# Sliding-window attention and a SiLU MLP on one core: transposes as 32x32 blocks on VectorE, matmuls in four small tiles

## The chip, the core and the metric

The kernel runs on one core of one Trainium2 chip. A core has TensorE (PE: matmuls, and its weight loads, PEld), VectorE (DVE), ScalarE (ACT), GpSimd (POOL) and SyncE (SP); POOL and SP issue DMAs to and from the chip's memory, POOL those that also cast float32 to bfloat16. Matmul results go to PSUM, here eight banks of 512 float32 for each of 128 partitions; everything else lies in SBUF. The metric is the device time of one execution in microseconds (us), as the median of several runs.

## The reference

Eight batches of eight heads, 576 positions, head size 64; a position attends to itself and the 63 before it. The result, all heads side by side, is the input of an MLP of 512, 2048 and 512 features.

```python
scores = scale * np.matmul(q, k.transpose(0, 1, 3, 2))          # scale = 1/8
mask = (rel >= 0) & (rel < window)                              # window = 64
scores = np.where(mask, scores, -1000000000.0)
attn = np.exp(scores - np.max(scores, axis=-1, keepdims=True))
attn = attn / (np.sum(attn, axis=-1, keepdims=True) + 1e-09)
x = np.matmul(attn, v).transpose(0, 2, 1, 3).reshape(B * S, H * D)   # 4608 x 512
h = x @ w_in
out = (h * (1.0 / (1.0 + np.exp(-h)))) @ w_out
```

## The kernel before

**Layout.** TensorE contracts over partitions, so q and k are needed with the head's 64 features on partitions (`qt`, `kt`), and the attention result O, which comes out with positions on partitions, must be turned again for the first MLP layer (`bridge`: features on partitions, 72 blocks of 64 positions). The kernel therefore transposes q, k and O, in three ways:

- Batch 0: `turn_first` (L294) transposes q and k on TensorE, `lift` copies them out of PSUM.
- Batch 1: `load_cast` loads a pair of heads (147 KB as bfloat16), `turn_twos` (L306, matmuls at L310) transposes on TensorE, `lift_twos` (L319) copies out in four quarters, on ACT or DVE.
- Batches 2 to 7 (`NX = 2`): `load_raw` loads pairs into `nat` (L259), `turn_raw` (L261) has SP issue a DMA that transposes two pairs into `tt`, and `spread` (L265) copies each quarter on DVE to its place, 32 copies per batch.
- O: `normal` (L385) divides by the row sums. Up to batch 2's second group, and in one group of batch 3, `back` (L388, matmuls at L390) transposes on TensorE and `to_bridge` (L399, L401) copies out; all other groups use `turn_o` (L393), a transposing DMA from SP.

**Attention.** A unit is one batch, three blocks of 64 queries (`g`, 0 to 2), and four heads (`a`, 0 or 1; "half") or all eight ("whole", batches 2 to 7). `scores` (L344, matmuls L350) multiplies 128 keys by 64 queries over 64 features; the two heads of a pair lie on partitions 0 to 63 and 64 to 127, so the array is used as two tiles of 64 rows. `expo` (L364) takes exp on ACT, `masking` (L367) multiplies by the window on DVE (in batch 0 a bias is added on TensorE instead, L358). `values` (L369, matmuls L373) has the 64 queries of two heads in two tiles of 64 columns, with a column of ones in `vv` for the row sum; `inverse` (L379) takes its reciprocal. `shift_v` (L333, L335) copies v so that each window of 128 keys has its own place.

**MLP.** Nine tiles of 512 positions. `first_layer` (L406): 16 groups of 128 features by 4 contractions; `silu` (L412) on ACT; `second_layer` (L415): 4 blocks of 128 positions by 16 contractions; `copy_out` (L421) and `store`. In tile 0 the first `FIRST = 6` groups are cut into 192 and 320 positions, since the first 192 are ready first, and the second layer takes the contractions in the outer loop, as w_out arrives.

**Order.** No order is written by hand: `Plan` (L12) is a planner that runs before the program is emitted. Each operation has a class with a rank, the engines that may take it with their estimated times, what it depends on, and the PSUM banks that it needs (`at` for scores, `pv` for values, `mp` for the MLP). The planner plays the program through with these times and emits each engine's operations in the order found; on the chip an engine executes its own in that order and waits where something is late. Scores are admitted by `scores_may_run` (L436): a whole unit only in a second layer with more than 14 of its 64 matmuls left. The DMA operations' times (`dma=`) are estimates of the same kind. `warm` (L668) keeps TensorE busy until the first batch's exps.

Of the kernel before, what the change touches and what calls it, by code (L numbers as in the profile page):

```python
# [14 lines left out]
class Plan:  # L15
# [12 lines left out]
    def add(self, cls, us, fn, deps=(), lat=0.08, gate=None, dma=None, pool=None, table=None, b=0, nb=1):  # L28
        if b > 1 and cls in ("cast", "lift", "spread", "mask", "norm"):
            lat = 0.2  # L30
        op = dict(us=us, first=self.rank[cls] + b if b or cls not in self.rank0 else self.rank0[cls], fn=fn, deps=[d for d in deps if d is not None], lat=lat, gate=gate, dma=dma,
                  pool=pool, table=table, seen=None, n=self.count, untils=[[] for _ in range(nb)], bank=[])
        self.count += 1
        self.queues.setdefault(cls, []).append(op)
        return op
# [87 lines left out]
def kernel(ctx, tc, q, k, v, w_in, w_out, out):  # L123
# [6 lines left out]
    NM = 6  # L130
    NR = S // NM
# [7 lines left out]
    NN, NNB, NTS, NE, NOT, NGT = 5, 8, 4, 12, 4, NFT + 3  # L139
    FIRST, EARLY_OUT = 6, 1  # L140
    FIRST_LOADS = [(x[0], int(x[1])) for x in "q0 k0 q1 k1 q2 q3 k2 k3 v0 v1 v2 v3".split()]
    NX, NXO = 2, 3
    NOX, NRC, NV = 4, 6, 3
# [18 lines left out]
    nats = [keep.tile([128, 2 * NM * 128], BF16, name=f"nat{i}") for i in range(NN)]  # L162
    tts = [keep.tile([128, 2 * S], BF16, name=f"tt{i}") for i in range(NTS)]
    natbs = [keep.tile([128, 2 * NM * D], BF16, name=f"natb{i}") for i in range(NNB)]
# [4 lines left out]
    rcs = [keep.tile([128, 2, 3], FP32, name=f"rc{i}") for i in range(NRC)]  # L169
    oxs = [keep.tile([128, 3, 2, 128], BF16, name=f"ox{i}") for i in range(NOX)]  # L170
# [10 lines left out]
        rank=dict(prime=-8, early=-10, one=-9, first=-9, dma=-1, ld0=-1, ld1=-1, st=-2, xo=-1.5, xk=-1.4, silu=-3, out=-2, pv=0, ot=0, s=1, moe=99, warm=200, turn=2,  # L181
                  norm=0, inverse=0, bridge=0, exp=1, mask=1, lift=2, spread=2, shift=2, cast=4, late=5, clear=9),
        rank0=dict(turn=-6, cast=-6, lift=-5, shift=-4.5, exp=-4, mask=-4, inverse=-3.5, norm=-3, bridge=-3.2),
        ahead=dict(s=-5.5, exp=-4.6, pv=-5.5, inverse=-4.3, norm=-4.2, ot=-5.5, bridge=-4.25),
# [44 lines left out]
    def head(pj, hh):  # L229
        return 4 * (pj // 2) + 2 * hh + pj % 2  # L230

    def pair(b, pj, kk):
        return (q, k)[kk][b, head(pj, 0):head(pj, 1) + 1:2]

    def two(u, kk):
        return (q, k)[kk][0, 2 * u:2 * u + 2].rearrange("h s d -> (h s) d").rearrange("(p m) d -> p (m d)", m=NM0)

    def load_cast(w, b, pj, kk):

        nc.gpsimd.dma_start(  # L240
            out=natbs[w][0:NR].rearrange("p (h y) -> p h y", h=2),
            in_=pair(b, pj, kk).rearrange("h (p m) d -> p h (m d)", m=NM),
        )
# [11 lines left out]
    def raw(i):  # L255
        return nats[i][0:NR].rearrange("p (j h y) -> p j h y", j=2, h=2)

    def load_raw(i, b, pj, kk):
        nc.gpsimd.dma_start(out=raw(i)[:, pj % 2], in_=pair(b, pj, kk).rearrange("h (p m) d -> p h (m d)", m=NM))  # L259

    def turn_raw(i, t):  # L261
        nc.sync.dma_start_transpose(  # L262
            out=tts[t].rearrange("x (m p) -> x m p", m=2 * NM), in_=nats[i][0:NR])

    def spread(e, t, b, pj, kk, hh, r):  # L265
        copies[e](  # L266
            out=place_one(b, pj, kk)[64 * hh:64 * hh + 64].rearrange("x (p m) -> x p m", m=NM)[:, :, r::2],
            in_=tts[t][64 * r:64 * r + 64].rearrange("x (j h m p) -> x j h p m", j=2, h=2, m=NM // 2)[:, pj % 2, hh],
        )
# [8 lines left out]
    def load_w_in(f):  # L278
        nc.gpsimd.dma_start(
            out=w_in_sb[:, :, f * 256:(f + 1) * 256],  # L280
            in_=w_in[:, f * 256:(f + 1) * 256].rearrange("(c p) f -> p c f", p=128),
        )
# [23 lines left out]
    def turn_twos(op, w):  # L306

        pst = at_bf16(op).rearrange("x (m p) -> x m p", m=NM)
        for m in range(NM):
            nc.tensor.matmul(  # L310
                pst[:, m], lhsT=natbs[w][0:NR, 128 * m:128 * m + 128], rhs=ident[0:NR, 0:NR],
                is_transpose=True, start=(m == 0), stop=(m == NM - 1),
            )

    def place_one(b, pj, kk):
        return kt[b % NK][:, 64 + pj * S:64 + (pj + 1) * S] if kk else qt[b % NK][:, pj * S:(pj + 1) * S]

    def lift_twos(e, op, b, pj, kk, hh, r):
        copies[e](  # L319
            out=place_one(b, pj, kk)[64 * hh:64 * hh + 64].rearrange("x (p m) -> x p m", m=NM)[:, :, r::2],  # L320
            in_=at_bf16(op)[64 * r:64 * r + 64].rearrange("x (h m p) -> x h p m", h=2, m=NM // 2)[:, hh],
        )
# [18 lines left out]
    def at_pv(bank):  # L341
        return banks[bank][:, 0:6 * (D + 1)].rearrange("k (j x y) -> k j x y", j=2, x=3)

    def scores(op, b, a, g, of):  # L344
        for j in range(2):
            for x in range(3):
                at = (2 * a + j) * S + (3 * g + x) * 64
                for hh in range(2):
                    r = slice(64 * hh, 64 * hh + 64)
                    nc.tensor.matmul(  # L350
                        at_six(of[hh])[:, j, x], lhsT=kt[b % NK][r, at:at + 128], rhs=qt[b % NK][r, at:at + 64],
                        start=(b > 0 and j == x == 0), stop=(j == 1 and x == 2),
                    )

    def scores_idle(op, b, a, g, of):

        for hh in range(2):
            nc.tensor.matmul(  # L358
                banks[of[hh]][:, 0:384], lhsT=ident,
                rhs=(bias0 if g == 0 else bias).rearrange("k x h i -> k (x h i)"), start=True, stop=False)  # L360
        scores(op, b, a, g, of)
# [6 lines left out]

    def values(bank, b, a, g, n):  # L369
        for j in range(2):  # L370
            for x in range(3):
                for hh in range(2):
                    nc.tensor.matmul(  # L373
                        at_pv(bank)[64 * hh:64 * hh + 64, j, x], lhsT=es[(2 * n + hh) % NE][:, j, x],
                        rhs=vv[b % NV][:, head(2 * a + j, hh) * NB + 3 * g + x, 0:D + 1],
                        start=(j == x == 0), stop=(j == 1 and x == 2),
# [5 lines left out]
    def ox(n):  # L382
        return oxs[n // 2 % NOX][:, :, n % 2].rearrange("k x (j d) -> k j x d", j=2)

    def normal(e, bank, n):  # L385
        nc.vector.tensor_mul(ox(n), at_pv(bank)[:, :, :, 0:D], rcs[n % NRC].unsqueeze(3).to_broadcast([128, 2, 3, D]))  # L386

    def back(bank, n):  # L388
        for x in range(3):
            nc.tensor.matmul(banks[bank][:, 128 * x:128 * x + 128], lhsT=oxs[n // 2 % NOX][:, x, n % 2], rhs=ident,  # L390
                             start=(x == 0), stop=(x == 2))

    def turn_o(n, b, g):  # L393
        n0 = b * NB + 3 * g
        nc.sync.dma_start_transpose(
            out=bridge[:, n0:n0 + 3].rearrange("x t (a h) i -> x (t a) (h i)", a=2),
            in_=oxs[n // 2 % NOX].rearrange("i t a x -> i (t a x)"))

    def to_bridge(e, bank, b, a, g):  # L399
        n0 = b * NB + 3 * g  # L400
        copies[e](out=bridge[:, n0:n0 + 3, 2 * a:2 * a + 2].rearrange("x t h i -> x t (h i)"),  # L401
                  in_=banks[bank][:, 0:384].rearrange("x (t y) -> x t y", t=3))
# [28 lines left out]
    nat_free, natb_free, tt_free, n_tt = {}, {}, {}, [0]  # L431
    g_pv, g_norm, g_back, g_mask, o_done = [], [], [], [], {}
# [15 lines left out]
    def add_first_batch():  # L448
        got = {}
        for what, u in FIRST_LOADS:  # L450
# [6 lines left out]
            if u == 0:  # L457
# [4 lines left out]
                nat_free[i] = ca  # L462
# [9 lines left out]
            for i in range(2):  # L472
# [3 lines left out]
                kq_done[(0, x)] = kq_done.get((0, x), []) + tu["untils"][i]  # L476
            for w in ws:
                natb_free[w] = tu
# [4 lines left out]
    def add_batch_qk(b):  # L483
        pool = "at"
        slot, parts = {}, {0: [], 1: []}
        for pj in range(NP):
            kq_done[(b, pj)] = []
        for pj in range(NP):
            busy = s_last.get((b - NK, pj), []) + ([c_k[b % NK]] if b < NK else [])
            for kk in range(2):  # L490
                if b >= NX:
                    if pj % 2 == 0:
                        slot[kk] = n_nat[0] % NN
                        n_nat[0] += 1
                    i = slot[kk]
                    parts[kk] += [p.add("dma", {"POOL": 0.66}, lambda _, i=i, pj=pj, kk=kk: load_raw(i, b, pj, kk),
                                        [nat_free.get(i)], dma=0.65, lat=MARGIN)]
                    if pj % 2 == 0:
                        continue
                    t = n_tt[0] % NTS  # L500
                    n_tt[0] += 1
                    x = p.add("xk", {"SP": 1.4}, lambda _, i=i, t=t: turn_raw(i, t), parts[kk] + tt_free.get(t, []), dma=2.2)
                    nat_free[i] = x
                    parts[kk], tt_free[t] = [], []
                    for y in (pj - 1, pj):
                        for hh, r in [(0, 0), (0, 1), (1, 0), (1, 1)]:
                            kq_done[(b, y)].append(p.add(
# [216 lines left out]
```

## Time and profile before

| | |
|---|---|
| median of 3 runs | 319.32 us (318.86 to 319.51) |
| the profiled execution, its own time | 313.79 us |
| its span, first to last instruction | 312.0 us |
| mean granted TensorE clock | 0.995 |
| busy: PE, DVE, ACT, POOL | 294.3, 156.0, 179.6, 85.1 us |
| moved by DMA | 38.53 MB |

The profile is of one execution. Its page gives each engine's busy time; the span in 40 slices of 7.8 us, each digit a share in tenths; groups of instructions by source line as "line engine operation, written<-read, shapes, count | busy us, mean ns of one | idle us before them and what ended it". The timeline gives start, duration and count of merged instructions, with the idle time before them in brackets. "PEclk" is the share of its full clock that TensorE was granted. The chain of waits is followed back from the last instruction.

### The profile page before, as it was taken

The page shows a single profiled execution, that of the slowest core. Times are in us where ns is not written, and L with a number is a line of the kernel's source. Part 1 is how long each engine was busy: PE and PEld are TensorE (multiplying, and loading weights), DVE is VectorE, ACT ScalarE, POOL GpSimd, SP SyncE. Part 2 cuts the span into 40 slices and gives each one's busy share as a digit, 9 for nine tenths or more (in the row PEclk, how much of TensorE's full clock was granted, in tenths as well). Part 3 has the DMA queues.
Part 4 walks back from the last instruction along what each step waited for, and adds up shares of the span by engine and source line. Part 5 has one row for each costly group of instructions (what it writes and reads, how often), then busy time and mean ns, then how long its engine had stood idle before and what let it go on. Part 6 is the DMA issues. An engine that isn't in the chain of part 4 may idle for free.

```text
span 312.0 us, 6619 instructions
## 1 busy us (share of the span) xinstructions
PE 294.3 (94%) x2603; PEld 145.9 (47%) x2633; DVE 156.0 (50%) x443; ACT 179.6 (58%) x330; POOL 85.1 (27%) x119
## 2 busy tenths in 40 slices
PE   4999989999979999999959999999999999999996
PEld 2566445444534454445424455445544444444444
DVE  2481776696599888986995188716500000000000
ACT  4788976666528753776346745775375146316611
POOL 8947846283260832095500000000000000000000
PEclk9999999999999999999979999999999999999999
DMA  8999999999999999999999033103320110010011
GB/s 165 167 197 182 165 203 161 160 276 156 156 235 171 157 185 177 174 223 148 191 200 196 3 109 99 33 0 97 84 59 2 67 67 3 34 67 34 2 65 69
DMA packets 102494, 38.53 MB, mean 123 GB/s; under 512 B 79680, under 2 KB 97728, under 8 KB 102464
## 3 DMA queue, kind: packets, MB, share of 16 engines
q0 software_dynamic: 56288, 18.06, 56.3%
q1 hardware_dynamic: 46176, 20.06, 32.9%
q8 instruction: 20, 0.33, 0.4%
q14 instruction: 10, 0.08, 0.1%
HBM read 36.70 MB, written 9.44 MB: 148 GB/s over the span
## 4 chain that ended last, share of the span: by engine, by line
PE 66%; DMA 24%; issue 3%; DVE 2%; POOL 2%; SPq 1%; ACT 0%; POOLq 0%; DVEq 0%; ACTq 0%
PE mp L406 32%; PE mp L415 27%; DMA vv<-in_v_dram 8%; DMA bridge<-ox 7%; DMA tt<-nat 3%; DMA nat<-in_q_dram 3%; DMA w_out_sb<-in_moe_w_out_dram 2%; PE mp L373 2%; PE at L350 2%; DMA natb<-in_q_dram 1%; POOL vv L273 1%; SPq L262 1%; PE at L300 1%; DVE ox L386 1%; PE mp L358 1%
## 5 line engine op out<-in xcount | busy, mean ns | idle before, releaser
L406 PE MATMUL mp<-bridge,w_in_sb 128*128 128x512 bf16 (+2 forms) x600 | 130.6, 372 | 3.7 <-DMA bridge<-ox 3.3
L415 PE MATMUL mp<-w_out_sb,g 128*128 128x512 bf16 (+2 forms) x578 | 128.9, 368 | 3.0 <-issue 2.2
L412 ACT ACTIVATE g<-mp 128x512 bf16<-128x512 f32 (+2 forms) x150 | 85.4, 580 | 36.3 <-PE mp L406 35.1
L406 PEld LDWEIGHTS <-w_in_sb 128*128 128x128 bf16 x600 | 57.6, 98 | 71.8 <-issue 8.3
L415 PEld LDWEIGHTS <-g 128*128 128x128 bf16 x608 | 55.5, 98 | 58.4 <-issue 0.5
L421 ACT COPY ot<-mp 128x512 f32<-128x512 f32 (+2 forms) x33 | 18.4, 560 | 62.7 <-PE mp L415 37.2
L364 ACT ACTIVATE e<-at 128x384 bf16<-128x384 f32 x88 | 36.8, 495 | 16.0 <-PE at L350 14.9
L367 DVE TENSOR_TENSOR e<-e,mask 128x384 bf16<-128x384 bf16 x84 | 26.9, 352 | 19.8 <-ACT e L364 19.3
L273 POOL DMA_DIRECT2D vv<-in_v_dram x32 | 32.6, 1026 | 8.8 <-DVE rc L380 4.7
L266 DVE COPY qt<-tt 64x288 bf16<-64x288 bf16 x96 | 33.6, 350 | 2.3 <-DMA tt<-nat 0.9
L266 DVE COPY kt<-tt 64x288 bf16<-64x288 bf16 x96 | 33.6, 350 | 1.8
L259 POOL DMA_DIRECT2D nat<-in_k_dram x24 | 15.6, 652 | 45.0 <-DMA tt<-nat 39.9
L386 DVE TENSOR_TENSOR ox<-mp,rc 128x384 bf16<-128x384 f32 x37 | 18.6, 542 | 0.2
L259 POOL DMA_DIRECT2D nat<-in_q_dram x24 | 15.8, 660 | 9.2 <-DMA tt<-nat 5.8
L373 PEld LDWEIGHTS <-e 128*64 128x64 bf16 x576 | 11.4, 110 | 10.5 <-issue 6.6
L350 PEld LDWEIGHTS <-kt 64*128 64x128 bf16 x576 | 10.2, 95 | 6.8 <-issue 4.7
L350 PE MATMUL at<-qt,kt 64*128 64x64 bf16 x528 | 13.0, 191 | 0.1
L380 DVE RECIPROCAL rc<-mp 128x6 f32<-128x6 f32 x37 | 6.8, 192 | 12.0 <-PE mp L373 11.9
L335 DVE COPY vv<-vv 64x576 bf16<-64x576 bf16 (+1 forms) x14 | 7.7, 549 | 6.6 <-DMA vv<-in_v_dram 6.1
L373 PE MATMUL mp<-vv,e 128*64 128x65 bf16 x444 | 10.7, 196 | 0.0
L412 ACT ACT_TABLE_LOAD x6 | 7.7, 1283 | 0.4 <-PE mp L406 0.3
L364 ACT ACT_TABLE_LOAD x6 | 7.7, 1283 | 0.1
(61 smaller groups left out, 123.1 us busy)
## 6 DMA issues: line engine op xcount, KB each, us to landing
out_dram<-ot SPq DMA_DIRECT2D x35, 256.0 KB, 2.2
vv<-in_v_dram POOLq DMA_DIRECT2D x32, 144.0 KB, 8.2
nat<-in_q_dram POOLq DMA_DIRECT2D x24, 144.0 KB, 8.6
nat<-in_k_dram POOLq DMA_DIRECT2D x24, 144.0 KB, 7.9
w_in_sb<-in_moe_w_in_dram POOLq DMA_DIRECT2D x8, 256.0 KB, 9.4
w_out_sb<-in_moe_w_out_dram POOLq DMA_DIRECT2D x8, 256.0 KB, 7.3
natb<-in_q_dram POOLq DMA_DIRECT2D x7, 144.0 KB, 6.2
natb<-in_k_dram POOLq DMA_DIRECT2D x7, 144.0 KB, 6.1
```

Of the source, the lines that this page charges most:

```text
L259: nc.gpsimd.dma_start(out=raw(i)[:, pj % 2], in_=pair(b, pj, kk).rearrange("h (p m) d -> p h (m d)", m=NM))
L266: copies[e](out=place_one(b, pj, kk)[64 * hh:64 * hh + 64].rearrange("x (p m) -> x p m", m=NM)[:, :, r::2], in_=tts[t][64 * r:64 * r + 64] ...
L273: queue[e].dma_start(out=vv[b % NV][:, 2 * g0 + 1:2 * g1 + 1:2, 0:D], in_=v[b].rearrange("h s d -> (h s) d").rearrange("(g p) d -> p g d", ...
L350: nc.tensor.matmul(at_six(of[hh])[:, j, x], lhsT=kt[b % NK][r, at:at + 128], rhs=qt[b % NK][r, at:at + 64], start=(b > 0 and j == x == 0), ...
L364: nc.scalar.activation(out=es[n % NE], in_=at_six(bank), func=ACTF.Exp, scale=scale)
L367: nc.vector.tensor_mul(es[n % NE], es[n % NE], mask0 if g == 0 else mask)
L373: nc.tensor.matmul(at_pv(bank)[64 * hh:64 * hh + 64, j, x], lhsT=es[(2 * n + hh) % NE][:, j, x], rhs=vv[b % NV][:, head(2 * a + j, hh) * N ...
L386: nc.vector.tensor_mul(ox(n), at_pv(bank)[:, :, :, 0:D], rcs[n % NRC].unsqueeze(3).to_broadcast([128, 2, 3, D]))
L406: nc.tensor.matmul(banks[bank["bank"][0]][:, lo:hi], lhsT=w_in_sb[:, c, ft * 128:(ft + 1) * 128], rhs=bridge[:, (j * TT + lo) // 64:(j * T ...
L412: nc.scalar.activation(out=gts[gt][:, lo:hi], in_=banks[bank["bank"][0]][:, lo:hi], func=ACTF.Silu)
L415: nc.tensor.matmul(banks[bank["bank"][0]][:, 0:hi - lo], lhsT=gts[gt][:, m * 128:(m + 1) * 128], rhs=w_out_sb[:, f, lo:hi], start=(f == 0) ...
L421: copies[e](out=ots[ot][:, lo:hi], in_=banks[bank["bank"][0]][:, 0:hi - lo])
```

## The change

- q and k of batches 1 to 7 are loaded by `load_four`: four heads at once, 128 partitions with 1152 consecutive elements (18 positions of 64 features) each, so that a head lies on a quarter of 32 partitions. `turn_blocks` turns 32x32 blocks on VectorE, half a load (576 elements) in each of two instructions per load. Then a head has 32 of its features (s = 0, 1) on its 32 partitions at a time.
- `scores` contracts 32 features twice, in four tiles of 32 rows, a head and a PSUM bank each: 48 matmuls per whole unit instead of 24.
- `values` takes 32 queries at a time in four tiles of 32 columns, a head each: also 48. O then has a head on 32 partitions, and `to_bridge` turns 32x32 blocks of it on VectorE, 384 elements, into `bridge`. This holds for batch 0 too.
- Gone: `load_cast`, `turn_twos`, `lift_twos`, `load_raw`, `turn_raw`, `spread`, `back`, `turn_o`, and with them all transposing DMAs and the batches' special ways.
- In `bridge` a partition now has features 2p and 2p + 1 of a half in the two places of that half, so w_in is loaded in the same order, in ten loads instead of eight.
- Batch 1 has whole units. FIRST is 8. The loads of batch 1's v and of w_out are issued in the order of `SECOND_LOADS`. Buffers: 8 `nat` of half the size, 6 `ox`.

The diff, cut to its core:

```diff
-    NN, NNB, NTS, NE, NOT, NGT = 5, 8, 4, 12, 4, NFT + 3
-    FIRST, EARLY_OUT = 6, 1
+    NN, NNB, NE, NOT, NGT = 8, 8, 12, 4, NFT + 3
+    FIRST, SECOND_LOADS = 8, "wvvwvv"
-    NX, NXO = 2, 3
-    NOX, NRC, NV = 4, 6, 3
+    NOX, NRC, NV = 6, 6, 3
...
+    def load_four(i, b, a, kk):
+        nc.gpsimd.dma_start(
+            out=nats[i], in_=(q, k)[kk][b, 4 * a:4 * a + 4].rearrange("h s d -> (h s d)").rearrange("(p x) -> p x", p=128))
+
+    def turn_blocks(i, b, a, kk, part):
+        n = NR // 2
+        to = kt[b % NK][:, 64:] if kk else qt[b % NK]
+        nc.vector.transpose(
+            out=to[:, 2 * a * S:2 * a * S + 2 * S].rearrange("x (s t r) -> x r s t", s=2, r=NR)[:, n * part:n * part + n],
+            in_=nats[i].rearrange("p (r s d) -> p r s d", r=NR, s=2)[:, n * part:n * part + n],
         )
...
-    def load_w_in(f):
+    def load_w_in(a, lo, hi):
         nc.gpsimd.dma_start(
-            out=w_in_sb[:, :, f * 256:(f + 1) * 256],
-            in_=w_in[:, f * 256:(f + 1) * 256].rearrange("(c p) f -> p c f", p=128),
+            out=w_in_sb[:, 2 * a:2 * a + 2, lo:hi],
+            in_=w_in[256 * a:256 * a + 256, lo:hi].rearrange("(p s) f -> p s f", s=2),
         )
...
+    def scores(op, b, g):
+        for s in range(2):
+            for a in range(2):
+                for x in range(3):
+                    at = (2 * a + s) * S + (3 * g + x) * 64
+                    for h in range(4):
+                        r = slice(32 * h, 32 * h + 32)
+                        nc.tensor.matmul(
+                            at_six(op["bank"][h])[:, a, x], lhsT=kt[b % NK][r, at:at + 128], rhs=qt[b % NK][r, at:at + 64],
+                            start=(s == a == x == 0), stop=(s == a == 1 and x == 2),
+                        )
...
     def values(bank, b, a, g, n):
-        for j in range(2):
-            for x in range(3):
-                for hh in range(2):
+        for x in range(3):
+            for t in range(2):
+                for h in range(4):
                     nc.tensor.matmul(
-                        at_pv(bank)[64 * hh:64 * hh + 64, j, x], lhsT=es[(2 * n + hh) % NE][:, j, x],
-                        rhs=vv[b % NV][:, head(2 * a + j, hh) * NB + 3 * g + x, 0:D + 1],
-                        start=(j == x == 0), stop=(j == 1 and x == 2),
+                        at_pv(bank)[32 * h:32 * h + 32, x, t], lhsT=e_of(b, a, n, h)[:, x, 32 * t:32 * t + 32],
+                        rhs=vv[b % NV][:, (4 * a + h) * NB + 3 * g + x, 0:D + 1],
+                        start=(x == t == 0), stop=(x == 2 and t == 1),
                     )
...
+    def to_bridge(n, b, a, g):
         n0 = b * NB + 3 * g
+        nc.vector.transpose(
+            out=bridge[:, n0:n0 + 3, 2 * a:2 * a + 2].rearrange("x t s (u i) -> x t s u i", u=2),
+            in_=oxs[n % NOX].rearrange("p t u (d s) -> p t s u d", s=2))
...
+                ld = p.add("dma", {"POOL": 0.66}, lambda _, i=i, a=a, kk=kk: load_four(i, b, a, kk), nat_free.get(i, []),
+                           dma=1.7, lat=MARGIN)
+                nat_free[i] = [p.add("block", {"DVE": 0.7}, lambda _, i=i, a=a, kk=kk, part=part: turn_blocks(i, b, a, kk, part),
+                                     [ld] + busy, b=b) for part in range(2)]
+                kq_done[(b, a)] += nat_free[i]
...
-        whole = b > 1
+        whole = b > 0
...
+            br = p.add("bridge" + first, {"DVE": 0.5}, lambda _, n=n, a=a: to_bridge(n, b, a, g), [no], b=b)
```

## The prediction

> **What bounds the kernel now.** I read the page first, busy shares and the slices of the span.
>
> ```profile
> PE 294.3 (94%) x2603; PEld 145.9 (47%) x2633; DVE 156.0 (50%) x443; ACT 179.6 (58%) x330; POOL 85.1 (27%) x119
> ...
> PE   4999989999979999999959999999999999999996
> ...
> DVE  2481776696599888986995188716500000000000
> ...
> DMA  8999999999999999999999033103320110010011
> ```
>
> TensorE is the bound: its row is full from the third slice on, with a dip in slice 12 (about 86 us) and in slice 21 (about 156 us). VectorE is at eight and nine tenths only up to slice 21, and the DMA engines are full exactly as long. So what counts is what TensorE executes, and its waits. The useful work is the two MLP layers:
>
> ```profile
> L406 PE MATMUL mp<-bridge,w_in_sb 128*128 128x512 bf16 (+2 forms) x600 | 130.6, 372 | 3.7 <-DMA bridge<-ox 3.3
> L415 PE MATMUL mp<-w_out_sb,g 128*128 128x512 bf16 (+2 forms) x578 | 128.9, 368 | 3.0 <-issue 2.2
> ```
>
> The 372 ns is the latency of one; in the chain of waits 64 of L406 take 13.99 us, 0.219 us each. The nine tiles need 1152 of these (some are cut in parts): 252 us. The first begins at 20.5, and 3 us follow the last. The other 36 us of the span are attention on TensorE, transposes on TensorE, and waits. The timeline of TensorE gives the waits:
>
> ```profile
> 40.97 0.41 PE L310 MATMUL at<-ident,natb 96*128 96x96 bf16 x6 [0.85 <-DVE kt L319]
> ...
> 88.01 0.34 PE L390 MATMUL mp<-ident,ox 128*128 128x128 bf16 x3 [1.88 <-DVE ox L386]
> ...
> 159.27 1.03 PE L406 MATMUL mp<-bridge,w_in_sb 128*128 128x512 bf16 x2 [3.29 <-DMA bridge<-ox]
> ```
>
> All three stand at things that the change replaces. The second is VectorE behind a late load of v (the chain has 16.8 us for that v load, from 68.78 on). The last also lowers the clock: windows, with the columns PE, PEld, DVE, ACT and POOL busy, clock, DMA share, GB/s:
>
> ```profile
> 155.00:170.00 15.00, 11.71 (x70) 5.20 (x70) 12.11 (x36) 7.73 (x12) 0.73 (x1) 0.89 1.52 196
> 170.00:185.00 15.00, 14.63 (x175) 7.34 (x176) 6.45 (x21) 9.92 (x20) 0.00 (x0) 1.00 0.24 56
> ```
>
> The list of waits tells why loads run to 170 us: buffers that wait for a transpose by DMA.
>
> ```profile
> POOL nat L259 <- DMA tt<-nat: 45.6, 10, 10.2
> ```
>
> [...] with transposes in flight, a load of v took 16.8 us where the median is 8.2. [...] The trace shows two abreast: in a prologue unit the two halves start at 15.00 and 15.00, 15.04 and 15.04, 15.06 and 15.07. Four abreast no run here shows. [...]
>
> **The change part by part.** The sum is made on the profiled execution, 313.79 us (span 312.0 and 1.8 around it). The median of the runs is 319.32, 5.5 above; I carry that offset unchanged.
>
> *TensorE work removed.* Turns of batch 1 (L310): 8 bursts, each 0.25 from its start to the next matmul: 2.0, and the 0.85 wait before the last. Turns of O (L390): 14 of the 18 groups lie after the first L406, each 0.17: 2.4. The 4 earlier ones and their copies lie in the prologue, replaced by VectorE below. Batch 1 has six half units now (scores 1.6, values 1.9 us in the burst starts) and then three whole ones. A whole unit costs 1.04: the tile from 192.74 to 224.90 has 32.16, less 128 x 0.219 = 28.0, over 4 units. 3.5 - 3.1 = 0.4.
>
> *Waits removed.* 1.88 and 3.29. And the clock: the 64 of L406 after the long wait take 15.45, where 14.0 is usual: 1.4. What is late next? A tile waits for the norm and one VectorE transpose in place of a DMA of 4.2 median and 12.5 at most, and in steady state units run ahead: when the fifth tile starts at 159.27, ten units of batches 2 to 4 have been scored and eight are needed. I expect nothing in that place.
>
> *VectorE.* Out: 192 copies L266 of 0.35 (67.2), its share of L319 (8.2) and L401 (3.4). In: 56 block turns of 576 elements and 48 bridge turns of 384. Price: [...] the estimates are 0.65 and 0.45 us. Sum 36.4 + 21.6 = 58, so VectorE falls from 156 to about 135. Bounds: [...] twice as slow if the writes 36 bytes apart halve it. Per later batch then: 8 x 0.65 turns, masks 12 x 0.35, inverses 6 x 0.19, norms 6 x 0.54, bridge turns 6 x 0.45, shifts 1.5: 18 us in 31 of TensorE, and 25 at the upper bound. So on the mean nothing, because 28 us of MLP per tile hide it; without that cover it would be 58 us. Queued behind a block turn that waits for its load are masks, and the values wait for those; a turn of 0.65 delays a mask by that much at most, against 3 to 4 us between score bursts.
>
> *Four tiles.* Scores and values are 48 matmuls each per unit instead of 24. Now 24 of L350 take 0.35 in 12 rounds of 29 ns, 24 of L373 in 12 rounds of 31. Four abreast is again 12 rounds: lower bound 0. Two abreast is 24 rounds: 12 x (29 + 31) ns x 21 units = 15.3 us. One at a time 46. I take four abreast with rounds some 2 ns longer: 1.0.
>
> *DMA.* The 24 + 15 transposes and their 10.0 MB of the 38.5 go, from SP, which then has only stores. q and k come in 4 loads per batch of twice the size, freed by VectorE instead of by a DMA; the 45.6 us of POOL's wait go. Before 48 us no transpose runs and DMA moves 165 to 200 GB/s, so the beginning gets no faster: the bytes up to batch 1 and w_out are the same. w_in in 10 loads instead of 8 costs POOL 2 x 0.75, behind which batch 1's loads stand; [...] From both: 0.4.
>
> *Prologue and first tile.* The last norm before the first L406 ends at 19.88; then come 0.35 on TensorE and a copy of 0.56. A transpose of 0.45 replaces both, but VectorE also takes the other half's copy, which ScalarE made: zero. FIRST = 8 cuts 8 matmuls more in two (101 + 136 instead of 219 ns): 0.15; it covers 3.2 us in which VectorE has four more norms and turns. Then the hand-over: first layer 20.5 + 14.6 + 0.3 = 35.4, second 14.0 + 3.1, so tile 1 could start at 52.5 (now 58.08). Batch 1's data are there at about 39 as now, units follow each other by 4.2 (179.82, 184.12, 188.21), so the third is scored at 47.4, and 5.8 later (exps and masks 2.5, values 0.5, inverses, norms, two turns 2.4, and waits) its last turn ends: 53.2. I take 1.0 as a new wait, from 0 to 3.5.
>
> Sum: 2.0 + 0.85 + 2.4 + 0.4 + 1.88 + 3.29 + 1.4 = 12.2 saved; 1.0 + 0.4 + 0.15 + 1.0 = 2.55 paid; 9.65 less. Profiled 304.1, median 309.7.
>
> **Rivals.** (1) The gain goes into new waits: TensorE's order is fixed by the planner, and where a VectorE turn comes later than planned, TensorE stands as it did at 88.01. For it: all three waits above are of this kind, and batch 1 as whole units leaves no slack in tile 0. Against: after tile 1 VectorE is lighter and units run ahead. With the hand-over at 3.5 and some 0.25 at each of 21 units: 8 given back, 317.5.
> (2) The small tiles do not run four abreast; this ends slower. Its place is the 42 bursts of scores and values. It decides when a round exceeds 29 to 31 by 10.65 us / (21 x 24 rounds) = 21 ns, at some 51 ns. Two abreast: 309.7 - 1.0 + 15.3 = 324.0. For it: column tiles of 32 and row tiles of 32 appear nowhere in this trace, and 8 instructions must issue in a round. Against: the pair's instructions start 1.5 to 4 ns apart in a 29 ns round, so eight fit.
> (3) The transposes on DMA were hidden and only the TensorE work counts: 2.0 + 0.85 + 2.4 + 0.4 - 2.55 = 3.1, 316.2. Against: the wait of 3.29 names one.
>
> **How the numbers follow.** Forecast 0.66 (303.5 to 314), rivals (1) and (3) together 0.17 (314 to 320), rival (2) 0.14 (over 320), more gain than I see 0.03. The range 303.5 to 319.0 leaves out some 0.18. The three runs differ by 0.2%, which is about what can be told from no change. Faster: 0.66 + 0.03 + 0.11 = 0.80; same 0.04; slower, rival (2) and the rest of (1), 0.16.
>
> **What would show it.** 48 of the scores' matmuls in 0.35 to 0.5 us, and the same for values; if 0.7 or more, rival (2). No wait of TensorE over 1 us after 60 us, clock 1.00 in every window from there; otherwise (1). VectorE's turns near 0.65 and 0.45, its total near 135. DMA idle from some 130 us or earlier, no POOL waits of 10 us. First L406 at 20 to 21, tile 1's first at 52.5 to 56. A much longer start of batch 1 (its scores after 42) would prove the DMA term wrong.

## The result, and the profile after

The changed kernel takes 354.45 us in the median of four runs (350.66 to 354.69); the kernel before took 319.41 beside it (318.86 to 320.95). The ratio is 1.106 (1.098 to 1.114): slower by a tenth, where 309.7 was forecast. An execution more than 1.5% above the fastest of the same kernel counts as slow, and the ratios leave such executions out, so they are not always the ratio of the medians. The profiled execution took 354.69 us, with a span of 352.9.

The page of the changed kernel, with the busy shares, the slices of the span, and the chain of waits by engine:

```profile
PE 305.3 (87%) x3619; PEld 147.8 (42%) x3619; DVE 233.8 (66%) x328; ACT 172.4 (49%) x311; POOL 65.1 (18%) x93
...
PE   5959456989406999699989998999999999999996
...
DVE  2648985999999699959998999699760262000000
...
PEclk9969969899855999789999998999999999999999
DMA  8999999363933192509451900100020011011002
...
PE 46%; DVE 28%; issue 11%; DMA 7%; POOL 6%; ACT 1%; POOLq 0%; DVEq 0%; ACTq 0%
```

VectorE was to fall from 156 to about 135 us; it rose to 233.8. It is mostly full from the eighth slice (62 us) to the 27th, and TensorE has a hole in slices 11 and 12 (88 to 106 us) and shallower ones before and after it. The DMA engines are full only in the first seven slices (to 62 us, where it was 171 before) and move 28.62 MB instead of 38.53, as the change says, and no wait of TensorE in this profile ends with a transfer. The groups of that page, with idle time and its releasers at the end of each row, tell what fills VectorE:

```profile
L371 PE MATMUL mp<-bridge,w_in_sb 128*128 128x512 bf16 (+2 forms) x608 | 130.5, 372 | 2.4 <-DVE ot L386 1.2
...
L247 DVE STREAM_TRANSPOSE qt<-nat 128x576 bf16<-128x576 bf16 x28 | 72.9, 2780 | 2.1 <-DMA nat<-in_q_dram 2.1
L247 DVE STREAM_TRANSPOSE kt<-nat 128x576 bf16<-128x576 bf16 x28 | 73.2, 2777 | 0.0
...
L351 PE MATMUL mp<-vv,e 128*32 128x65 bf16 x888 | 13.8, 200 | 22.4 <-DVE e L342 21.8
...
L365 DVE STREAM_TRANSPOSE bridge<-ox 128x384 bf16<-128x384 bf16 x48 | 24.8, 553 | 0.1
...
L333 PE MATMUL at<-qt,kt 32*128 32x64 bf16 x1008 | 13.0, 196 | 9.0 <-DVE kt L247 8.6
```

The bridge turns have nearly the forecast size: their median distance is 0.49 us from start to start, where 0.45 was forecast. A block turn has 2.78 us as its own latency and 2.47 from one start to the next, not 0.65; the 56 of them take 138 us, not 36. The MLP's matmuls are unchanged at 372 ns. The timeline of the changed kernel around the largest hole (start, duration, engine, instruction, count; in brackets the idle time before it and what ended it) shows how VectorE's time becomes TensorE's:

```profile
87.13 0.55 PE L333 MATMUL at<-qt,kt 32*128 32x64 bf16 x48
...
88.72 5.11 DVE L247 STREAM_TRANSPOSE qt<-nat 128x576 bf16<-128x576 bf16 x2
89.20 1.64 ACT L339 ACTIVATE e<-at 128x384 bf16<-128x384 f32 x4
93.48 5.27 DVE L247 STREAM_TRANSPOSE kt<-nat 128x576 bf16<-128x576 bf16 x2
...
98.40 5.27 DVE L247 STREAM_TRANSPOSE qt<-nat 128x576 bf16<-128x576 bf16 x2
...
103.32 5.27 DVE L247 STREAM_TRANSPOSE kt<-nat 128x576 bf16<-128x576 bf16 x2
...
108.24 1.33 DVE L342 TENSOR_TENSOR e<-e,mask 128x384 bf16<-128x384 bf16 x4
...
108.83 1.63 PE L351 MATMUL mp<-vv,e 128*32 128x65 bf16 x48 [16.73 <-DVE e L342]
```

The exps of a unit of batch 2 are done at 90.8. Its masks are emitted behind eight block turns of batch 3, which last 19.5 us; the planner counted 0.7 us for each, 5.6. TensorE stands 16.73 us before the values can start. The windows of the changed kernel, with busy PE, PEld, DVE, ACT, POOL, clock, DMA share and GB/s, give the price in clock as well:

```profile
90.00:110.00 20.00, 3.18 (x42) 1.46 (x43) 19.57 (x12) 1.43 (x4) 4.45 (x7) 0.63 0.83 92
110.00:125.00 15.00, 15.00 (x272) 7.29 (x261) 11.99 (x24) 4.72 (x11) 1.41 (x2) 0.81 0.23 58
```

TensorE is busy throughout the second window, at 0.81 of its clock. Over the whole span its stops of more than 0.1 us between matmuls sum to 39.9 us (9.6 before), and it is busy for 11 us more (305.3 against 294.3) although its transposes are gone; in run 2 below, with the same matmuls and a mean clock of 0.989 instead of 0.932, it is busy for 292.1. To within 0.4 us the longer stops (30.3) and the 11 us make the 40.9 by which the span grew. The list of waits of the changed kernel (waiter, what it waited for, total, count, longest) has them by cause:

```profile
POOL nat L240 <- DVE kt L247: 38.1, 8, 7.0
...
PE mp L351 <- DVE e L342: 21.8, 4, 16.7
...
PE at L333 <- DVE kt L247: 8.6, 1, 8.6
...
PE at L351 <- issue: 6.8, 2, 4.3
```

Three of these are VectorE's turns: the buffers that POOL waits for are now held by turns instead of by transposing DMAs, the masks stand behind turns, and batch 1's first scores wait 8.6 us for a turn of k at 39 us. The last is of another kind: nothing that the profile shows was awaited. The experiments take up both.

### The profile page after: what moved, and what is told of

It is laid out like the page before. It is cut to its first block, busy times and chain, and to the rows that moved or that the text cites. A ratio compares the mean times of both kernels' runs of the same rounds, so it can differ in the third digit from the quotient of the medians.

```text
span 352.9 us, 8322 instructions
## 1 busy us (share of the span) xinstructions
PE 305.3 (87%) x3619; PEld 147.8 (42%) x3619; DVE 233.8 (66%) x328; ACT 172.4 (49%) x311; POOL 65.1 (18%) x93
## 2 busy tenths in 40 slices
DMA packets 52965, 28.62 MB, mean 81 GB/s; under 512 B 38848, under 2 KB 44608, under 8 KB 52928
## 4 chain that ended last, share of the span: by engine, by line
PE 46%; DVE 28%; issue 11%; DMA 7%; POOL 6%; ACT 1%; POOLq 0%; DVEq 0%; ACTq 0%
PE mp L380 26%; PE mp L371 15%; DVE qt L247 13%; DVE kt L247 11%; DMA vv<-in_v_dram 3%; DMA nat<-in_q_dram 3%; PE mp L351 3%; POOL vv L254 2%; PE at L333 2%; POOL w_in_sb L260 2%; DVE ox L361 1%; DVE bridge L365 1%; POOL natb L230 1%; DVE e L342 1%; POOL nat L240 1%
## 5 line engine op out<-in xcount | busy, mean ns | idle before, releaser
L380 PE MATMUL mp<-w_out_sb,g 128*128 128x512 bf16 (+2 forms) x608 | 138.6, 385 | 0.0
L377 ACT ACTIVATE g<-mp 128x512 bf16<-128x512 f32 (+2 forms) x152 | 86.0, 575 | 40.9 <-PE mp L371 39.8
L247 DVE STREAM_TRANSPOSE qt<-nat 128x576 bf16<-128x576 bf16 x28 | 72.9, 2780 | 2.1 <-DMA nat<-in_q_dram 2.1
L247 DVE STREAM_TRANSPOSE kt<-nat 128x576 bf16<-128x576 bf16 x28 | 73.2, 2777 | 0.0
L351 PE MATMUL mp<-vv,e 128*32 128x65 bf16 x888 | 13.8, 200 | 22.4 <-DVE e L342 21.8
L351 PEld LDWEIGHTS <-e 128*32 128x32 bf16 x1152 | 12.8, 98 | 40.8 <-DVE e L342 26.7
L365 DVE STREAM_TRANSPOSE bridge<-ox 128x384 bf16<-128x384 bf16 x48 | 24.8, 553 | 0.1
L333 PE MATMUL at<-qt,kt 32*128 32x64 bf16 x1008 | 13.0, 196 | 9.0 <-DVE kt L247 8.6
L240 POOL DMA_DIRECT2D nat<-in_k_dram x14 | 7.8, 554 | 46.5 <-DVE kt L247 37.5
L333 PEld LDWEIGHTS <-kt 32*128 32x128 bf16 x1008 | 10.2, 96 | 13.8 <-DVE kt L247 8.7
L240 POOL DMA_DIRECT2D nat<-in_q_dram x14 | 7.8, 554 | 35.9 <-DVE qt L247 19.4
L351 PE MATMUL at<-vv,e 128*32 128x65 bf16 x264 | 4.1, 201 | 6.8 <-issue 6.8
```

What stands on the lines that cost most here:

```text
L247: nc.vector.transpose(out=to[:, 2 * a * S:2 * a * S + 2 * S].rearrange("x (s t r) -> x r s t", s=2, r=NR)[:, n * part:n * part + n], in_=n ...
L333: nc.tensor.matmul(at_six(op["bank"][h])[:, a, x], lhsT=kt[b % NK][r, at:at + 128], rhs=qt[b % NK][r, at:at + 64], start=(s == a == x == 0 ...
L351: nc.tensor.matmul(at_pv(bank)[32 * h:32 * h + 32, x, t], lhsT=e_of(b, a, n, h)[:, x, 32 * t:32 * t + 32], rhs=vv[b % NV][:, (4 * a + h) * ...
L365: nc.vector.transpose(out=bridge[:, n0:n0 + 3, 2 * a:2 * a + 2].rearrange("x t s (u i) -> x t s u i", u=2), in_=oxs[n % NOX].rearrange("p ...
L377: nc.scalar.activation(out=gts[gt][:, lo:hi], in_=banks[bank["bank"][0]][:, lo:hi], func=ACTF.Silu)
L380: nc.tensor.matmul(banks[bank["bank"][0]][:, 0:hi - lo], lhsT=gts[gt][:, m * 128:(m + 1) * 128], rhs=w_out_sb[:, f, lo:hi], start=(f == 0) ...
```

## Experiments

Theory W: a block turn is slow because it writes two bytes at a time, each 36 bytes from the last (18 positions are interleaved in `to`). Rival P: the slow turn alone would be borne; the time is lost because the order was made with 0.7 us for it. Later, theory F, on TensorE's stops that wait for nothing. Each comparison has its own runs of the kernel before, whose median was 316.1 to 319.4, so ratios are given beside times.

**1. The turn by itself.** A kernel with VectorE operations on 576 elements only, in six rounds of one execution; it has no attention and no MLP and writes zeros. `e` is the distance of two successive writes in elements.

```diff
+def to_step(t, e, n=18): return t[:, 0:32 * n].rearrange("x (u t e) -> x u e t", u=n // e, e=e)
+for _ in range(6):
+    nc.vector.transpose(out=to_step(to, 1), in_=rows(nat, 1))     # and e = 2, 3, 6, 9, 18
+    nc.vector.tensor_copy(out=to_step(to, 2), in_=rows(nat, 2))   # and 6, 18
+    nc.vector.transpose(out=to_step(to4, 1), in_=rows(nat4, 1))   # four bytes; and 2, 6, 18
```

> Only the disputed instruction, on an otherwise idle core, six times in a row each: VectorE block turns of 576 bfloat16 elements with the writes 2, 4, 6, 12, 18 and 36 bytes apart, plain copies with 4, 12 and 36 bytes, turns of 576 four-byte elements with 4, 8, 24 and 72 bytes, and one turn that reads 36 bytes apart and writes without gaps. It computes nothing of the reference; the output is zeros. Theory W (the distance between writes sets the price): 0.65 us at 2 bytes, rising to about 2.47 from one start to the next at 36 bytes, and the plain copy at 36 bytes is as slow as the turn. Rival T (turning itself is slow from a loaded tile, whatever the writes): all six bfloat16 turns near 2.47 and the copies near 0.65. A third outcome, W only in the full program because of other engines' traffic: all near 0.65 here.

The groups of this run: L34 to L39 are the two-byte turns with distances of 2, 4, 6, 12, 18 and 36 bytes, L41 and L42 plain copies with 12 and 36 bytes, L43 and L46 four-byte turns with 4 and 72 bytes (the mean is the latency of one):

```profile
L34 DVE STREAM_TRANSPOSE to<-nat 128x576 bf16<-128x576 bf16 x6 | 4.6, 766 | 4.9 <-DMA nat<-in_q_dram 4.8
...
L35 DVE STREAM_TRANSPOSE to<-nat 128x576 bf16<-128x576 bf16 x6 | 4.8, 799 | 0.1
...
L37 DVE STREAM_TRANSPOSE to<-nat 128x576 bf16<-128x576 bf16 x6 | 12.5, 2080 | 0.1
...
L39 DVE STREAM_TRANSPOSE to<-nat 128x576 bf16<-128x576 bf16 x6 | 15.8, 2631 | 0.1
...
L41 DVE COPY to<-nat 128x576 bf16<-128x576 bf16 x6 | 12.4, 2062 | 0.1
...
L42 DVE COPY to<-nat 128x576 bf16<-128x576 bf16 x6 | 8.3, 1391 | 0.1
...
L43 DVE STREAM_TRANSPOSE to<-nat 128x576 f32<-128x576 f32 x6 | 4.9, 815 | 0.0
...
L46 DVE STREAM_TRANSPOSE to<-nat 128x576 f32<-128x576 f32 x6 | 7.8, 1303 | 0.0
```

W holds for the turn: it costs 0.66 to 0.85 us from start to start with writes 2 or 4 bytes apart, and 2.2 to 2.7 with 36. No other engine computes here, and the price is 2.7 also after 30 us, when the DMA engines are idle too. It is not the transposing as such: a plain copy with 12 bytes is as slow as the turn. But the copy with 36 bytes takes half the time of the turn, which I had not expected, so the price is not one of distance alone. The turn that reads 36 bytes apart and writes without gaps takes 1.04 to 1.24 us: stepping on the reading side costs too, but much less. Four-byte writes suffer less: 576 of them 72 bytes apart take 1.06 to 1.28 us, twice the data in half the time.

**2. Writes without gaps.** One letter order in `turn_blocks`; the same instructions and the same number of matmuls, but q and k land in another order of positions, so attention is over wrong positions.

```diff
-out=to[...].rearrange("x (s t r) -> x r s t", s=2, r=NR)[...]
+out=to[...].rearrange("x (s r t) -> x r s t", s=2, r=NR)[...]
```

> The changed kernel with one edit: the block turns of q and k write without gaps, so positions lie in another order within a head; attention is over the wrong positions, the amount of work is the same. Theory W: a turn 0.65 us instead of 2.47, VectorE's total about 132 us instead of 234, no wait of TensorE on a mask over 1 us after 60 us, time 310 to 316 (the forecast 309.7 plus the 4.3 us stop of TensorE in the prologue that the changed kernel's trace shows as issue). Rival T: the same 354. Rival F (the doubled number of small matmuls costs the time): over 340 with a fast turn.

308.25 us (307.61 to 308.46), ratio 0.981 (0.974 to 0.988). In the groups of this run a turn is back near the forecast's size (0.66 us from start to start):

```profile
L247 DVE STREAM_TRANSPOSE qt<-nat 128x576 bf16<-128x576 bf16 x28 | 19.8, 747 | 3.7 <-DMA nat<-in_q_dram 3.7
```

In its list of waits nothing of TensorE is left over 1 us but two stops at L351, the start, and a wait in the prologue:

```profile
PE at L351 <- issue: 4.7, 2, 2.4
PE at L581 <- POOL ident L189: 4.2, 1, 4.2
PE at L313 <- DVE kt L291: 1.1, 1, 1.1
PE at L333 <- ACT e L339: 0.6, 3, 0.2
```

VectorE is busy for 135.0 us, the number forecast; from its page:

```profile
PE 292.1 (96%) x3619; PEld 143.1 (47%) x3619; DVE 135.0 (44%) x328; ACT 171.9 (56%) x311; POOL 66.0 (22%) x93
```

So the distance of the writes is the cause of the loss; how it becomes a loss of 45 us is the question of runs 3 and 4. The rest of the forecast's sum came out to within 3.5 us: the span is 305.8, where the forecast had 302.3. The time lies just below the 310 to 316 that were expected.

**3. The planner is told the truth.** The changed kernel, its slow turns included, with their measured price in the plan. With that price alone the planner finds no order, so the gate of whole units is loosened too.

```diff
-            return not whole and rest > 0 and not p.done(op["deps"])
+            return rest > 0 and not p.done(op["deps"])
-                nat_free[i] = [p.add("block", {"DVE": 0.7}, ...
+                nat_free[i] = [p.add("block", {"DVE": 2.47}, ...
```

> The changed kernel, but the planner is given 2.47 us for a block turn instead of 0.7, and a whole unit may be admitted while the first layer waits; the program is the same work in another order. Rival P (the turns fit, only the order made with 0.7 is wrong): below 325, and the masks' wait of 16.7 us gone. Theory W with VectorE as the bound: turns and VectorE's total stay (234 us), the long wait is split into smaller ones, 335 to 352.

323.77 us (323.23 to 324.48), ratio 1.032 (1.022 to 1.042): what P expected, not what W did, though the kernel is still slower than the one before. VectorE is as loaded as in the changed kernel (235.4 us), but the planner now puts single turns between the masks of a batch, and rows of four or five where no mask waits. The longest wait of TensorE for a mask is 2.3 us (list of waits of this run):

```profile
PE at L351 <- DVE e L342: 2.3, 1, 2.3
```

**4. The gate alone.** To see which of the two edits of run 3 did it.

```diff
-            return not whole and rest > 0 and not p.done(op["deps"])
+            return rest > 0 and not p.done(op["deps"])
```

> The changed kernel with one edit only, that the planner may start batch 1's and later whole units wherever their data are ready (the gate as in the run with the price 2.47), while a block turn still counts 0.7 us in the plan. Theory P (the wrong price makes the order bad): masks still stand behind rows of block turns, 345 to 358 us, with at least one wait of TensorE for masks over 8 us. Theory G (the gate, not the price, brought the 31 us): 320 to 330 us. I expect P.

351.25 us (350.27 to 355.75), ratio 1.105 (1.094 to 1.115), as the changed kernel, with the long wait for masks again (list of waits of this run):

```profile
PE mp L351 <- DVE e L342: 21.8, 4, 16.7
```

The gate alone brings nothing, so it was the price, with the gate that it needs. Of the loss, 27 to 31 us is the order made with the wrong price (351.3 or 354.5 less 323.8; by the ratios, which allow for the different runs of the kernel before, some 23), and another 15.5 the long turns themselves even in a good order (323.8 less 308.3).

**5. Turns of four-byte words.** Two neighbouring features are turned as one word, so a turn has 288 words, and the scores read q and k with a step of two elements. (The empty columns ahead of k double with it, which the cut leaves out.)

```diff
-            out=to[...].rearrange("x (s t r) -> x r s t", s=2, r=NR)[:, n * part:n * part + n],
-            in_=nats[i].rearrange("p (r s d) -> p r s d", r=NR, s=2)[:, n * part:n * part + n],
+            out=to[...].bitcast(FP32).rearrange("x (t r) -> x r t", r=NR)[:, n * part:n * part + n],
+            in_=nats[i].bitcast(FP32).rearrange("p (r w) -> p r w", r=NR)[:, n * part:n * part + n],
-                    at = (2 * a + s) * S + (3 * g + x) * 64
+                    at = 2 * a * S + (3 * g + x) * 128 + s
-  lhsT=kt[b % NK][r, at:at + 128], rhs=qt[b % NK][r, at:at + 64],
+  lhsT=kt[b % NK][r, at:at + 255:2], rhs=qt[b % NK][r, at:at + 127:2],
```

> The changed kernel with block turns over four-byte words (two features at a time): half as many elements, 288 per turn, written 72 bytes apart; scores then read q and k in steps of 4 bytes. The result is the reference's. Theory W with a price per write: 288 x 4.3 ns = 1.24 us per turn, VectorE about 165 us, 315 to 322. If the price goes by bytes or grows with the distance: turns of 2.4 us, 350. Rival on TensorE: if reading in steps of 4 bytes slows it, score bursts go from 0.48 to 0.9 and 9 us are added.

307.58 us (305.13 to 309.44), ratio 0.979 (0.967 to 0.991). The groups of this run have the turn:

```profile
L247 DVE STREAM_TRANSPOSE qt<-nat 128x288 f32<-128x288 f32 x28 | 17.5, 703 | 3.4 <-DMA nat<-in_q_dram 3.2
```

The expectation was too high: it priced a write at 4.3 ns, while 576 words had taken 1.06 to 1.28 us in run 1; a turn now has 288, and takes 0.54 from start to start. A burst of scores is no slower for the step of two (0.48 us in both, 189 ns mean in L333 against 190 in run 2). This is the change as it was meant, with a turn no dearer than the forecast's.

**6 to 8. How long may a turn be?** Each four-byte turn is issued twice, with the price 0.7 (run 6) or with 1.3 and the loosened gate (run 7), or four times with 0.7 (run 8).

```diff
+        for _ in range(2):     # 4 in run 8
             nc.vector.transpose(
```

> The kernel with four-byte turns, each turn issued twice in a row to the same place; the planner still counts 0.7 us, and the result stays the reference's. This is the prediction's upper bound (turns twice as slow) put on the chip. If the mean load is what counts, as the prediction argued (25 us of VectorE per batch against 31 of TensorE), at most 1 us over word_turns' 307.6. Order theory (what stands in VectorE's queue ahead of a mask counts): eight turns ahead of a mask take 9.9 us instead of the planned 5.6, TensorE stands up to 4 us per batch at values, 312 to 325.

> The same doubled turns, but the planner counts 1.3 us for them (and may admit a whole unit while a first layer waits). Order theory: most of word_twice's loss comes back, 307 to 312. If VectorE's load itself costs the time: the same as word_twice.

> The kernel with four-byte turns, each turn issued four times in place of once, so that a turn costs some 4 x 0.62 = 2.5 us on VectorE, as in the changed kernel, but with writes of four bytes; the planner still counts 0.7 us. Theory L (only the length of the turn and the order matter): as the changed kernel, 340 to 358 us, masks waiting over 8 us behind turns. Rival M (single bytes-pairs written far apart also hold up other engines' access to SBUF): clearly less, 312 to 332 us. Twice the length cost only some 2 us, so the loss has to set in between twice and four times. I expect L.

Twice: 309.65 us (308.41 to 311.55), ratio 0.989 (0.975 to 1.003). Twice and told: 309.07 (307.89 to 311.45), ratio 0.987 (0.976 to 0.999), no difference that these runs show. Four times: 374.89 (374.03 to 376.34), ratio 1.182 (1.174 to 1.190). The timeline of run 6, at the place that answers to the changed kernel's hole, has eight doubled turns in a row ahead of the masks too (from 69.45 us; the last four here), but they end in time:

```profile
74.64 2.74 DVE L248 STREAM_TRANSPOSE qt<-nat 128x288 f32<-128x288 f32 x4
77.22 2.75 DVE L248 STREAM_TRANSPOSE kt<-nat 128x288 f32<-128x288 f32 x4
79.81 1.14 DVE L343 TENSOR_TENSOR e<-e,mask 128x384 bf16<-128x384 bf16 x4
...
80.21 1.33 PE L352 MATMUL mp<-vv,e 128*32 128x65 bf16 x48 [0.34 <-DVE e L343]
```

In run 8 it is the changed kernel's picture, with four-byte writes:

```profile
112.89 5.76 DVE L248 STREAM_TRANSPOSE kt<-nat 128x288 f32<-128x288 f32 x8
...
118.49 1.14 DVE L343 TENSOR_TENSOR e<-e,mask 128x384 bf16<-128x384 bf16 x4
...
118.90 1.62 PE L352 MATMUL mp<-vv,e 128*32 128x65 bf16 x48 [19.48 <-DVE e L343]
```

So the length of the turns is enough for the loss, and nothing further about two-byte writes is needed to explain it. Eight doubled turns of 1.3 us pass, eight of 2.5 or 2.8 don't. I had expected a clear loss in run 6, which did not come, and 340 to 358 in run 8, where it was 375: two of its turns take 5.6 us (112.89 to 118.49), so one costs 2.8 and not 2.47. By the forecast's own account of a batch (18 us of VectorE, 5.2 of them turns) the rest is 12.8; with eight turns of 0.65 it is 18, of 1.3 it is 23, of 2.47 it is 32.6, of 2.8 it is 35, against 31 of TensorE. The first two lie under the 31 and the last two over it. This is an estimate, and these three runs change load and queue together; it is runs 3 and 4 that tell the two apart.

**9 and 10. TensorE's own stops.** In runs 2 and 5 and in the changed kernel TensorE stops twice with no one to wait for. The timeline of run 5 (the 24 values of a group, cut in two):

```profile
16.51 0.29 PE L351 MATMUL at<-vv,e 128*32 128x65 bf16 x13
20.33 0.35 PE L351 MATMUL at<-vv,e 128*32 128x65 bf16 x11 [3.53 <-issue]
...
47.11 0.46 PE L351 MATMUL at<-vv,e 128*32 128x65 bf16 x35
50.27 0.38 PE L351 MATMUL at<-vv,e 128*32 128x65 bf16 x13 [2.70 <-issue]
```

In all three kernels the stops come after the same number of TensorE instructions, 703 and 1471 recorded matmuls and weight loads, so 768 apart. (One expectation counts two more, two synchronizing instructions at the start.) The trace lists DMA queues for instructions. One (q8) has 28 packets and 0.46 MB, so 16 KB each, beside 7238 recorded matmuls and weight loads of the changed kernel, and 20 packets beside 5236 in the kernel before: some 260 to a packet, if they are all for TensorE, which the trace does not say. In the changed kernel packets of this queue start at 18.92 and 58.23, during the two stops (of 4.26 and 2.52 us), and take 0.89 and 0.94 us; TensorE goes on 1.60 and 1.38 us after each has ended. Theory F: the stops belong to the count of TensorE's instructions, and not to a time or a place in the code. Bursts of small matmuls stand around both; 48 of these and their weight loads, 96 instructions, pass in 0.49 us. To move the count to another place in the code, 32 tiny matmuls (64 instructions) are put ahead, at the start of the warm-up (run 9) or ahead of the first MLP matmul (run 10):

```diff
+    shifted = []
     def warm(op):              # run 10: first_layer
+        for _ in range(0 if shifted else 32):
+            nc.tensor.matmul(banks[op["bank"][0]][:, 0:64], lhsT=ident, rhs=ident[:, 0:64], start=True, stop=True)
+        shifted.append(1)
```

> The kernel with four-byte turns, with 32 small matmuls (64 TensorE instructions, weight loads counted) added before the first load has landed, where TensorE is idle. Theory F [...]: the stops come again after the 705th and the 1473rd TensorE instruction of the trace, so 64 instructions earlier in the program, in other bursts; the second one gets shorter. Rival (the stop belongs to the place, a semaphore or the weights of that values burst): the stops stay at the same matmul, which is then the 769th and the 1537th. Time 305 to 310 in both.

> The kernel with four-byte turns, with the 32 tiny matmuls (64 TensorE instructions) ahead of the first MLP matmul in place of ahead of the warm-up. Theory F [...]: the first stop stays at the 703rd recorded instruction, 2 to 4 us at some 17 us, and the second, at the 1471st some 47 us, falls to under 1 us or goes; 303.5 to 307 us. Rival T (the stops belong to a time or to a place in the code, a late semaphore for instance): the first stop stays and the second too, 64 instructions later, at the 1535th; 306.5 to 309 us. I expect F.

Run 9: 302.48 us (301.31 to 304.46), ratio 0.966 (0.955 to 0.977). Run 10: 305.38 (304.55 to 306.90), ratio 0.963 (0.956 to 0.970); its runs of the kernel before are others, so the two ratios don't order them. The timeline of run 9:

```profile
17.46 0.24 PE L351 MATMUL at<-vv,e 128*32 128x65 bf16 x6
18.43 0.33 PE L351 MATMUL at<-vv,e 128*32 128x65 bf16 x18 [0.73 <-issue]
```

And that of run 10:

```profile
16.86 0.29 PE L351 MATMUL at<-vv,e 128*32 128x65 bf16 x13
19.54 0.27 PE L351 MATMUL at<-vv,e 128*32 128x65 bf16 x11 [2.38 <-issue]
```

The first stop stays at the 703rd instruction in both. In run 9 that is 64 instructions earlier in the program, and the stop is 0.73 us; in run 10 it is the old place, and 2.38. At the old place of the second stop TensorE does not stop in either run. At its old count, behind the 735th matmul in the order of the kernel, TensorE waits 0.18 us in run 9 and 0.63 in run 10; the profile puts both waits down to VectorE, so they decide nothing. But run 3, whose order differs, stops at the 703rd and the 1471st instruction too, and the second time in front of scores instead of values:

```profile
61.79 0.24 PE L333 MATMUL at<-qt,kt 32*128 32x64 bf16 x4 [1.03 <-issue]
```

So where the stops come, they follow the count and not the code. The first comes behind the 703rd instruction in ten kernels, the changed one and runs 2 to 10, with 0.73 to 4.37 us; the timelines of seven of these have the second too, with 1.03 to 3.05 us. That TensorE waits there for its next instructions is the author's reading of the two packets of the changed kernel; it is not shown, and why the stop in run 9 is shorter stays open.

Run 9 has the lowest median and the shortest span (301.6 us; 302.8 in run 10), and came out below the 305 to 310 expected. Both intervals lie below 1 (0.977 at most), so these versions are faster than both kernels. Which of the two is better is not shown, and that the stops fall well here is luck: nobody placed the instructions for it, and the next edit can move them.

## Why the prediction was wrong

**The step that failed is the price of a block turn**, under "VectorE": 0.65 us, with "twice as slow if the writes 36 bytes apart halve it" as the upper bound. Measured 2.47, 3.8 times the price and almost twice the bound. The price was the author's estimate; what the trace of the kernel before shows near it is a copy of 288 elements in 350 ns (L266), which at the same rate makes 0.70 us for 576. The price is right for writes without gaps (0.66 us in run 2) and was taken over to writes 36 bytes apart. The place was seen, but its bound was a guess. Two-byte turns with a step of 36 bytes take 3.9 to 4.6 ns an element, and four-byte turns with 72 bytes 1.8 to 2.2 ns a word (run 1). Measuring the instruction by itself would have turned the forecast.

**Two conclusions fell with it.** "On the mean nothing", as VectorE has 25 us per batch at most against 31: with 2.47 it has 32.6 (run 3 still loses 15.5 us in a good order). And "a turn of 0.65 delays a mask by that much at most": a row of eight turns stood ahead of the masks, as the planner's order allows. At 0.54 to 1.3 us per turn such a row is harmless (runs 5 to 7), so the statement was wrong even where its consequence was right. The planner holds the same wrong price (0.7), and this cost more than the turns' own load (runs 3 and 4).

**What held.** The TensorE terms and the four tiles: 48 scores take 0.48 to 0.49 us where 24 took 0.46, 48 values 0.49 against 0.50, so four tiles run abreast and rival (2) falls. The waits at 88 and 159 us and the lost clock are gone in runs 2 and 5, with no wait over 1 us and a full clock after 60 us, so the DMA transposes were not hidden and rival (3) falls; by time alone narrowly, since its 316.2 is a ratio of 0.990 and run 2's interval ends at 0.988. VectorE's 135 us, met in run 2. The bridge turns: 0.49 for 0.45. Batch 1's loads: its first scores start at 39.08 (36.94 in run 2), not after 42, though in the changed kernel most of them then wait for a turn until 47.91. Two signs did not come even in run 2: the last load lands at 160 us and not by 130, and POOL waits up to 24.9 us for a buffer of v. No stop of TensorE there hangs on either.

**Rival (1)** named the mechanism, a VectorE turn that comes later than planned, but gave it 8 us, which would have left the kernel faster at 317.5; the miss was 45 (354.45 against 309.7).

**What the sum lacked.** The span of run 2 is 3.5 us over the forecast's 302.3, with two stops of TensorE at L351, 4.7 in all, in it; run 9, which has nearly none, has a span of 301.6. The hand-over of tile 0 hung on these: tile 1 starts at 59.96 in run 2 but at 55.73 in run 9, within the 52.5 to 56 forecast (71.67 in the changed kernel, where the wait of 8.6 for a turn of k comes on top). The beginning of the changed kernel was late as well, 22.58 for the first MLP matmul where 20 to 21 was forecast, with a stop of 4.26 ahead of it. As a ratio to the kernel before the forecast was 0.970 (309.7 to 319.32); run 5 had 0.979 (0.967 to 0.991) and run 9 had 0.966 (0.955 to 0.977). Two of its sums are slightly off: two tiles abreast would add 15.1 us, not 15.3, and VectorE at its upper bound has 26 us per batch with both kinds of turn doubled, or 23 with the block turns alone, not 25. Neither bears on the result.

## What to carry to other kernels

Price an instruction by its access pattern, and measure it by itself if the pattern is new: here a transposing write that scattered single two-byte elements cost nearly four times one without gaps (2.47 us against 0.66), and turning pairs of elements as four-byte words removed the loss (0.54). Where an order is made ahead from estimated times, a wrong estimate can cost more than the slow instruction itself (here 23 to 31 us against 15.5): compare the estimates with the first trace, and ask how many of the suspect instructions can stand in a row ahead of something urgent. An engine with slack at one price may be the bound at another; work out at which price that turns.

## What the runs showed of the hardware that I had not expected

- In run 1 the cost of scattered two-byte writes follows no simple rule: 576 of them take 1.8 to 2.1 us at 12 bytes, 2.3 to 2.7 at 18 and 2.2 to 2.7 at 36 for the turn, while a plain copy takes 1.7 to 2.1 at 12 and 1.0 to 1.4 at 36.
- TensorE stops for 2.3 to 4.3 us, waiting for nothing that the profile shows, after its 703rd and its 1471st recorded instruction in the changed kernel and in runs 2 and 5, where bursts of small matmuls (96 instructions in 0.49 us) stand around these places. In the changed kernel it goes on 1.60 and 1.38 us after a 16 KB packet of instructions has ended; that it waits for these is not shown. With 64 instructions inserted ahead of the warm-up, one stop shrank to 0.73 us and the other went; the median was 302.48 us instead of 307.58, in another round of runs.
